# Second layer of a two-MLP kernel: 34 sets by seven block products instead of 17, one written order per kind of set, its weights decoded earlier

## The chip, the cores and the metric

The kernel runs on one core of a Trainium2 chip. The time is the device time of one execution in microseconds (us). The kernel before took 1127.06 us in the median of three runs (1126.33 to 1127.07). The engines are named as in the profile: PE (TensorE), PEld (its weight loads), DVE (VectorE), ACT (ScalarE), POOL (GpSimd) and SP (the engine whose queue starts most DMAs).

## What is computed

```python
def reference(**kw):
    X = np.fft.rfft(x, axis=1)                       # x: 2 x 3008 x 256
    x = np.fft.irfft(X * (filt_r + 1j * filt_i)[None], n=3008, axis=1)
    x = x.reshape(6016, 256)
    gate = 1.0 / (1.0 + np.exp(-(x @ moe_w_gate)))   # 256 -> 1536
    x = (gate * (x @ moe_w_val)) @ moe_w_out         # 1536 -> 256
    h = x @ moe2_w_in                                # 256 -> 2048
    return (h / (1.0 + np.exp(-1.702 * h))) @ moe2_w_out   # 2048 -> 256
```

A spectral filter comes first, then a gated layer (the first layer), then a layer with a sigmoid-GELU (the second layer). The weights arrive as float64 and are decoded on the chip.

## The kernel before

Precision: every fp32 operand is split into a high part (an fp32r copy, made by ACT) and a low part (the rest, made by a subtraction on POOL or DVE). `mm3` (lines 127 to 130) multiplies two split operands with three matmuls: high by high, high by low, low by high. A "product" below means these three matmuls, on a 128x128 block of weights and up to 512 columns of tokens.

Second layer: the 6016 tokens are twelve column tiles, ten of 512 and two of 448 columns (`tiles2`), taken as six pairs (p = 0 to 5). The 2048 hidden features are eight double blocks of 256 (fp = 0 to 7). A set is one pair p with one double block fp, so there are 48 sets. Into the hidden features each set goes by seven products instead of eight, P0 to P6 in the order P0, P4, P5, P1, P6, P2, P3 (`prod` in the loop, from line 1990 on): a Strassen-Winograd scheme, whose sums of weights and of tokens are made ahead. They lie in PSUM banks x (products 0, 5, 6, 3), y (4, 2) and z (1). ACT copies out c1 (from x) and c5 (from y). DVE then makes y = x + c5 (line 2011, here called Ay), z = z + c1 (line 2013, Az) and w = x + c5 (line 2025, Aw), and x is complete after P3. The GELU of z, w, y and x follows on ACT, once rounded (the high part) and once in full, and then the low part.

Out of the hidden features a set goes in one of two ways. A regular set (R) uses eight products (`Block.back`). A set by seven (S, class `Seven`, line 1817 on) uses seven, m1 to m7, with more sums: T1 = y - z, T3 = w - y, T2 = w - T1, T4 = x - T2, each split again into high and low. Of the seven, m3, m2 and m4 add into the accumulators. The products m1, m6, m7 and m5 go one after the other into one more bank, the chain, and after each DVE adds the chain into a sum in SBUF (k1 to k4, lines 1884 and 1886). At the end of a pair the sums are folded into the accumulators (`fold`, line 1919). `SETS7` names the sets by seven: fp 0, 2, 4, 6 in pairs 2 to 4, fp 4 and 6 in pair 1, fp 0, 2, 4 in pair 5, none in pair 0, which makes 17. Each is followed by an R set. The products of a set's second half are spread over the next set's first half.

Other work in this layer ("side steps") is taken from a list at places of the loop (`spend`, `rate`): the token forms of the next pair (four subtractions on DVE, seven high parts on ACT, seven low parts on DVE), the sums of output weights for the S sets (`out_sums`), and in pair 0 what is left of the decoding of the weights. The engines run their instructions in the order in which the program issues them; PE, DVE, ACT and POOL each go by this written order.

First layer: pairs p = 2 to 5 are run as twelve sets each by seven products in and eight out (line 1560 on). Decoding of the second layer's weights (`decode_chores`, 13 jobs here) begins in pair 4 and goes on into the second layer's pair 0.

Of the kernel before, what the change touches and what calls it, by code (L numbers as in the profile page):

```python
# [17 lines left out]
P = 128  # L18
# [71 lines left out]
def kernel(  # L90
# [29 lines left out]
    ascr = dram.tile([2, P, P], F32, name="ascr")  # L120

# [91 lines left out]
    def decode_chores(j, st, place):  # L213
# [4 lines left out]
        def start():  # L218
            t["raw"], _, _, own = raws.pop(0)
            slots.append(own)  # L220
            t["lw"], t["hw"] = t["raw"][:, :, 0], t["raw"][:, :, 1]
            ex = st.tile([P, 512], U32, tag="ex", name="ex")
            nc.vector.tensor_single_scalar(ex, t["hw"], 0x7FF00000, op=ALU.bitwise_and)
            t["c"] = st.tile([P, 512], I32, tag="c", name="c")
            nc.scalar.activation(out=t["c"], in_=ex, func=AF.Relu, bias=ebias, scale=8.0)
            t["m"] = st.tile([P, 512], U32, tag="m", name="m")
            nc.vector.tensor_scalar(t["m"], t["hw"], 0xFFFFF, 0x100000, op0=ALU.bitwise_and, op1=ALU.bitwise_or)
# [14 lines left out]
        def value():  # L242
            nc.vector.scalar_tensor_tensor(
                out=t["f"], in0=t["f"], scalar=2.0**-20, in1=t["c"].bitcast(F32), op0=ALU.mult, op1=ALU.mult
            )
            nc.scalar.activation(out=hi, in_=t["f"], func=AF.Copy)
# [34 lines left out]

        low.apart = end.apart = True
        return [start, mant, sign, value] + ([low] if j % 2 else [lambda: sums(0), low, lambda: sums(1), end])
# [899 lines left out]
    OUT = {(1, 0): 4, (1, 1): 6, (1, 2): 0, (1, 7): 2}  # L1183
# [290 lines left out]
    def forms_chores(dst, n, raws, spread, ahead, eng4=nc.vector):  # L1474
        def make():
            fs = Forms(dst, n, raws, spread, [st.tile([P, 512], F32, tag=k, name="xs") for k in ("ex", "c", "m")])
            cell.append(fs)
            one, two, three, four = fs.sums(eng4)
            if len(ahead) == 7:
                ks = (0, 1, 4, 5, 2, 6, 3)  # L1480
                steps = [one, two, three, four, lambda: fs.hi(0)]
                for k, nxt in zip(ks, ks[1:]):
                    steps += [lambda k=nxt: fs.hi(k), lambda k=k: fs.lo(k)]
                return steps + [lambda: fs.lo(3)]
# [33 lines left out]
    def l1_back(t, f, c, gp):  # L1518
# [3 lines left out]
        def run():  # L1522
            mm3(acc, [w[:, f, c * P:(c + 1) * P] for w in wo], [g[:, :n] for g in gp], f == 0, f == FC1 - 1)
            if f == FC1 - 1:
# [3 lines left out]
                evac(o[:, c, :n], acc, c)  # L1528
# [14 lines left out]
    def next_decode(j):  # L1543
        return decode_chores(j, st, lambda: [w[:, j % NWL] for w in wl] + [sp])

    def spend(q, n):
        for k in range(n):
            if not q and bulk and not hold_back:
                q.extend(next_decode(bulk.pop(0)))
            elif not q and out_jobs:  # L1550
                q.extend(out_sums(out_jobs.pop(0)))
# [8 lines left out]
    for p in range(FIRST, nt // 2):  # L1560
        n = tiles[2 * p][3]
        rhs = [[h[:, :n] for h in d] for d in sets[p]]
        for f in range(FC1):
# [32 lines left out]
            rate = (1, 0, 2) if first_set else RATE[p] if p == FIRST or f > 2 else (0, 2, 1) if f else (0, 0, 1)  # L1596
# [94 lines left out]
    frees = list(gring)  # L1691

    spares = []

    def gtake():
        return frees.pop(0)

    def give(slot, p):
        if p and slot is gring[0]:
            assert not spares  # L1700
            spares.extend(work.tile([P, 512], F32, tag=f"g{i}", name="spare", bufs=4) for i in range(2))
        else:
            frees.append(slot)

# [7 lines left out]
    class Block:  # L1712
        def __init__(self, i, j, p, fp, bank):
            self.i, self.j, self.t, self.fp, self.bank = i, j, 2 * p + j, fp, bank
            self.n = tiles2[self.t]
            self.own = p == 0 and i == 0 and (fp > 0 or j == 0)
            self.sg = None

        def take(self):
            self.slot = gtake()  # L1720
            self.gp = [x[:, :self.n] for x in self.slot]

        def hold(self):
            self.sg = work.tile([P, 512], F32, tag="sg", name="sg")[:, :self.n]
            return self.sg

        def act(self):
            self.take()
            if self.own:
                self.sg = self.bank  # L1730
            elif self.sg is None:
                self.hold()
            nc.scalar.activation(out=self.gp[0], in_=self.bank, func=AF.Gelu_apprx_sigmoid)  # L1733
            nc.scalar.activation(out=self.sg, in_=self.bank, func=AF.Gelu_apprx_sigmoid)  # L1734

        def full(self):
            nc.scalar.activation(out=self.bank, in_=self.bank, func=AF.Gelu_apprx_sigmoid)  # L1737
            self.sg = self.bank

        def high(self):  # L1740
            self.take()
            nc.scalar.activation(out=self.gp[0], in_=self.sg, func=AF.Copy)

        def low(self, eng=None):
            eng = eng or (nc.vector if self.own else nc.gpsimd)
            eng.tensor_sub(self.gp[1], self.sg, self.gp[0].bitcast(F32))  # L1746

        def back(self, c):
            t, n, f = self.t, self.n, 2 * self.fp + self.i
            end = self.fp == FC2 // 2 - 1 and self.i != self.j  # L1750
            acc = accs[self.j][c][:, :n]
            mm3(acc, wp(f, c), self.gp, opens(t, c), end, skip_group_check=True)
            if c:
                give(self.slot, now[0])
            if end:
                if c == 0:
                    outs[t, 2] = new_raw()
                o = outs[t, 2][:, c, :n]
                if c == 1 and t == nt - 2:
                    h = n // 2  # L1760
                    nc.scalar.copy(o[:, :h], acc[:, :h])
                    nc.scalar.dma_start(out=out[c * P:(c + 1) * P, pos2[t]:pos2[t] + h], in_=o[:, :h])
                    nc.vector.tensor_copy(o[:, h:], acc[:, h:])
                    nc.sync.dma_start(out=out[c * P:(c + 1) * P, pos2[t] + h:pos2[t] + n], in_=o[:, h:])
                    return
                evac(o, acc, c)
                (nc.scalar if t == nt - 1 and c == 0 else nc.sync).dma_start(
                    out=out[c * P:(c + 1) * P, pos2[t]:pos2[t] + n], in_=o
                )

    sout = [
        [wo[i][:, FC1 - 1, :P] for i in range(2)],
        [wo[i][:, FC1 - 1, P:] for i in range(2)],
        [sx0[i][:, 5, :] for i in range(2)],
    ]

    def load_sout(fp, *ks):
        q = SEVEN.index(fp)
        for k in ks:
            for i in range(2):  # L1780
                nc.sync.dma_start(out=sout[k][i].bitcast(F32), in_=oscr[q, i, :, k * P:(k + 1) * P])

    def out_sums(fp):
        w = slot(2 * fp + 1)
        q = SEVEN.index(fp)
        one, two = ("ex", "c") if q % 2 == 0 else ("c", "ex")
# [21 lines left out]
        def low():  # L1808
            if fp not in SETS7[nt // 2 - 1]:
                for i in range(2):  # L1810
                    nc.sync.dma_start(out=ascr[i], in_=w[i][:, P:2 * P].bitcast(F32))
            lo = st.tile([P, 512], F32R, tag=one, name="wlo")
            nc.vector.tensor_sub(lo, t["r"].rearrange("p k m -> p (k m)"), t["hi"].bitcast(F32))
            for i, x in enumerate((t["hi"], lo)):
                nc.sync.dma_start(out=oscr[q, i], in_=x[:, P:].bitcast(F32))
                nc.sync.dma_start(out=w[i][:, P:2 * P].bitcast(F32), in_=x[:, :P].bitcast(F32))

        steps = [lambda fn=fn: fn() for fn in (whole, sums, more, high, low)]
        for step in steps:
# [283 lines left out]
```

## Time and profile of the kernel before

| what | value |
|---|---|
| median of three runs | 1127.06 us |
| profiled execution | 1128.34 us, of which the span from the first to the last instruction is 1126.5 us |
| PE busy | 1117.2 us, 99% of the span, 5021 matmuls |
| DVE, ACT, POOL busy | 835.4, 672.8, 442.3 us |
| granted TensorE clock | 0.999 of full speed over the whole span |
| second layer on PE | from 644.5 to about 1122.5 us |

Matmuls overlap: a matmul of 512 columns is shown as 0.39 us long, but in a dense stretch the next one starts 0.227 us after it. DVE and ACT instructions overlap in the same way by about 0.1 us. So the time that PE loses is read from the distances between starts of matmuls, not from the busy share.

### The profile page before, as it was taken

Reading aid. Unit: us, or ns where it says so; the run is one execution under the profiler, and the core shown is the slowest. Engines: PE = TensorE matmul, PEld = TensorE weight load, DVE = VectorE, ACT = ScalarE, POOL = GpSimd, SP = SyncE. Lnnn points to the kernel's source line nnn. Section 1 sums busy time; section 2 is a strip of 40 time slices with the busy share of each in tenths; the row PEclk is TensorE's granted clock in tenths of the full one; section 3 lists DMA queues with packets and bytes.
Section 4 is the critical chain, followed back from the end, with each engine's and each line's share of the span. In section 5 each row is a group of like instructions: output and inputs, shape, how many; then the busy total and the mean of one; then the engine's idle time right before and its main releaser. Section 6 shows DMA issues by size and latency. Waiting matters only on the chain.

```text
span 1126.5 us, 15228 instructions
## 1 busy us (share of the span) xinstructions
PE 1117.2 (99%) x5021; PEld 895.8 (80%) x5021; DVE 835.4 (74%) x1395; ACT 672.8 (60%) x1276; POOL 442.3 (39%) x368
## 2 busy tenths in 40 slices
PE   9999999999999999999999999999999999999998
PEld 4378887767888888888888878888788888888897
DVE  6989997777688755787788789657876676776653
ACT  4555555554455544655565576667676666676664
POOL 3810003654333211211211132256566665666564
PEclk9999999999999999999999999999999999999999
DMA  8755238794300210026057251031030120210200
GB/s 208 202 183 182 94 113 220 184 194 85 94 1 1 70 41 1 19 108 126 1 184 246 85 183 39 1 117 47 15 116 20 43 75 15 85 29 20 66 15 33
DMA packets 101582, 100.29 MB, mean 89 GB/s; under 512 B 41024, under 2 KB 73536, under 8 KB 101504
## 3 DMA queue, kind: packets, MB, share of 16 engines
q1 hardware_dynamic: 99536, 96.42, 30.2%
q10 hardware_dynamic: 1968, 2.91, 0.8%
q8 instruction: 39, 0.64, 0.2%
q14 instruction: 39, 0.32, 0.1%
HBM read 62.34 MB, written 32.51 MB: 84 GB/s over the span
## 4 chain that ended last, share of the span: by engine, by line
PE 90%; DVE 2%; DMA 1%; ACT 1%; SPq 1%; POOL 1%; issue 1%; ACTq 0%; DVEq 0%; POOLq 0%
PE ps L128 30%; PE ps L130 29%; PE ps L129 29%; PE ps L328 2%; DMA fi<-in_fd_dram 0%; SPq L377 0%; DMA yraw<-tt 0%; DMA x<-in_xd_dram 0%; POOL g L1746 0%; DMA f<-fi 0%; DVE z L504 0%; ACT sg L1734 0%; DVE yp L1136 0%; SPq L363 0%; ACT ps L1737 0%
## 5 line engine op out<-in xcount | busy, mean ns | idle before, releaser
L1746 POOL TENSOR_TENSOR g<-sg,g 128x512 fp32r<-128x512 f32 (+1 forms) x82 | 113.2, 1382 | 141.9 <-ACT sg L1734 109.7
L125 POOL TENSOR_TENSOR g<-sg,g 128x512 fp32r<-128x512 f32 (+1 forms) x47 | 59.5, 1267 | 257.2 <-ACT g L124 257.2
L128 PE MATMUL ps<-yp,wg 128*128 128x512 f32 (+2 forms) x382 | 149.8, 393 | 0.0
L130 PE MATMUL ps<-yp,wg 128*128 128x512 f32 (+2 forms) x382 | 147.8, 387 | 0.0
L129 PE MATMUL ps<-yp,wg 128*128 128x512 f32 (+2 forms) x382 | 147.7, 387 | 0.0
L129 PE MATMUL ps<-g,wo 128*128 128x512 f32 (+1 forms) x305 | 117.4, 386 | 0.0
L128 PE MATMUL ps<-g,wo 128*128 128x512 f32 (+1 forms) x305 | 117.4, 386 | 0.0
L130 PE MATMUL ps<-g,wo 128*128 128x512 f32 (+1 forms) x305 | 117.3, 386 | 0.0
L1746 POOL TENSOR_TENSOR wo<-sg,wo 128x512 fp32r<-128x512 f32 (+1 forms) x65 | 89.1, 1371 | 64.6 <-ACT sg L1734 56.3
L128 PEld LDWEIGHTS ps<-yp,wg 128*128 128x128 f32 x382 | 71.7, 188 | 26.1 <-issue 13.0
L130 PEld LDWEIGHTS ps<-yp,wg 128*128 128x128 f32 x382 | 71.7, 188 | 14.3
L129 PEld LDWEIGHTS ps<-yp,wg 128*128 128x128 f32 x382 | 71.7, 188 | 13.1 <-issue 0.2
L1733 ACT ACTIVATE g<-ps 128x512 fp32r<-128x512 f32 (+1 forms) x73 | 43.1, 591 | 61.1 <-DVE ps L2013 58.0
L1637 ACT ACTIVATE sg<-ps 128x480 f32<-128x480 f32 (+1 forms) x48 | 28.1, 586 | 71.0 <-DVE ps L1635 71.0
L1671 DVE TENSOR_TENSOR g<-ps,g 128x480 fp32r<-128x480 f32 (+1 forms) x48 | 32.4, 675 | 48.8 <-ACT g L1668 48.6
L128 PEld LDWEIGHTS ps<-g,wo 128*128 128x128 f32 x305 | 57.2, 188 | 11.6 <-issue 0.8
L130 PEld LDWEIGHTS ps<-g,wo 128*128 128x128 f32 x305 | 57.2, 188 | 11.1
L129 PEld LDWEIGHTS ps<-g,wo 128*128 128x128 f32 x305 | 57.2, 188 | 10.9
L1734 ACT ACTIVATE sg<-ps 128x512 f32<-128x512 f32 (+1 forms) x103 | 60.5, 587 | 0.2 <-POOL g L1746 0.2
L2011 DVE TENSOR_TENSOR ps<-ps,tabs 128x512 f32<-128x512 f32 (+1 forms) x48 | 32.9, 685 | 37.0 <-PE ps L130 36.7
L128 PE MATMUL ps<-yp,sx 128*128 128x512 f32 (+2 forms) x129 | 50.2, 389 | 0.1
L1656 ACT ACTIVATE sg<-ps 128x480 f32<-128x480 f32 (+1 forms) x48 | 28.1, 586 | 37.2 <-PE ps L130 37.0
(372 smaller groups left out, 3144.3 us busy)
## 6 DMA issues: line engine op xcount, KB each, us to landing
yscr<-tt SPq DMA_DIRECT2D x56, 128.0 KB, 2.2
raw<-in_w_out_dram SPq DMA_DIRECT2D x14, 512.0 KB, 4.0
yraw<-xscr SPq DMA_DIRECT2D x14, 512.0 KB, 5.2
x<-in_xd_dram SPq DMA_DIRECT2D x32, 192.0 KB, 3.8
wscr<-wl SPq DMA_DIRECT2D x24, 256.0 KB, 2.0
wg<-wscr SPq DMA_DIRECT2D x24, 256.0 KB, 2.9
out_dram<-yraw SPq DMA_DIRECT2D x20, 256.0 KB, 2.1
f<-in_fd_dram SPq DMA_DIRECT2D x23, 192.0 KB, 4.3
```

The source lines that it names most:

```text
L125: lo_eng.tensor_sub(dst_lo, src, dst_hi.bitcast(F32))
L128: nc.tensor.matmul(out=o, lhsT=w[0], rhs=x[0], start=first, stop=False, **kw)
L129: nc.tensor.matmul(out=o, lhsT=w[0], rhs=x[1], start=False, stop=False, **kw)
L130: nc.tensor.matmul(out=o, lhsT=w[1], rhs=x[0], start=False, stop=last, **kw)
L328: nc.tensor.matmul(out=o[c], lhsT=w[64 * r:64 * r + n], rhs=x(r, k), start=True, stop=True, tile_position=(64 * r, 64 * k),)
L1637: nc.scalar.activation(out=sgz, in_=z, func=AF.Sigmoid)
L1656: nc.scalar.activation(out=sgy, in_=y, func=AF.Sigmoid)
L1671: nc.vector.tensor_sub(g0[1], x, g0[0].bitcast(F32))
L1733: nc.scalar.activation(out=self.gp[0], in_=self.bank, func=AF.Gelu_apprx_sigmoid)
L1734: nc.scalar.activation(out=self.sg, in_=self.bank, func=AF.Gelu_apprx_sigmoid)
L1746: eng.tensor_sub(self.gp[1], self.sg, self.gp[0].bitcast(F32))
L2011: nc.vector.tensor_add(y, x, s5[:, :n])
```

## The change

1. `SETS7` becomes fp 0 to 5 in pair 1 and fp 0 to 6 in pairs 2 to 5: 34 sets, most of them one behind the other. The block sums of output weights are made for seven double blocks (`OUT`: six in pair 0, the seventh in pair 1), and there is a second buffer for those that an S set loads (`souts`).
2. The loop of the second layer is rewritten. Each set is a table of single steps (`Set.ops`), and five written lines (`LINES`) give the order in which steps of the set before (with a "-"), of the current set, of the pair's end and side steps (aD, aA, aQ: the next one for DVE, ACT, POOL) are issued. The key is the kinds of the two sets: SS is an S set after an S set. One line covers one "frame": what is issued between one set's start and the next's. In names like `zhi`, `zf`, `zlo`: high part, full value, low part; `xf-` is that of the set before.
3. The low parts of the token forms move from DVE to POOL (`lo_eng`, aQ). At the end of a pair, POOL adds two pairs of sums (V, W), and DVE adds accumulator and sum into the output tile (e11 to e22).
4. The second layer's weights are decoded from pair 3 of the first layer on (its fourth), not pair 4; one job of thirteen is left for the second layer. ACT's table for GELU is called for ahead of the second layer.

The core of the diff:

```diff
-    SEVEN = (0, 2, 4, 6)
-    SETS7 = {1: (4, 6), 2: SEVEN, 3: SEVEN, 4: SEVEN, 5: (0, 2, 4)}
+    SEVEN = tuple(range(FC2 // 2 - 1))
+    SETS7 = {0: (), 1: (0, 1, 2, 3, 4, 5), 2: SEVEN, 3: SEVEN, 4: SEVEN, 5: SEVEN}
-    OUT = {(1, 0): 4, (1, 1): 6, (1, 2): 0, (1, 7): 2}
+    OUT = {(0, 2): 0, (0, 3): 1, (0, 4): 2, (0, 5): 3, (0, 6): 4, (0, 7): 5, (1, 7): 6}
...
-            if p == 3 and f == 10:
+            if p == 3 and f == 0:
                 raw_job(EARLY)
-            if p == 4 and f == 0:
                 raw_job(EARLY + 1)
+            if p == 3 and f == 1:
                 bulk += range(EARLY, NJ)
-            hold_back = p == 4 and f > 7 or p == 5 and f > 6
+            hold_back = p in (3, 4) and f > 7 or p == 5 and f > 7
...
+    gelu(warm, ebias)
+    LINES = {
...
+        "RS": (
+            "P0 bz0- bz1- c1 P4 xf- P5 c5 xlo- aQ P1 Ay bw1- ylo- aQ V W Az P6 zf P2 Aw bw0- yf bx1- T1 whi aA aA "
+            "bx0- wf e21 zhi P3 e11 by0- T2 xhi by1- T3 aD e22 e12"
+        ),
+        "SS": (
+            "zlo- xf- wlo- P0 T1hi- P4 T2hi- c1 m1- T2lo- T4- c5 xlo- m3- T3hi- aA k1- aD P5 T4hi- T3lo- aQ P1 Ay "
+            "m6- T1lo- Az P6 k2- zhi P2 zf Aw m7- T4lo- yf m2- whi k3- wf P3 T1 m5- T3 xhi T2 m4- k4-"
+        ),
...
+            ops["Ay"], ops["Az"], ops["Aw"] = add(y, x, c5), add(z, z, c1), add(f["w"], x, c5)
+            gelu_of("z", "z", z, f["z"], pool)
+            gelu_of("w", "w", f["w"], f["w"], pool)
+            if self.seven:
+                so = souts[nseven % 2]
+                nseven += 1
+                for k in (2, 0, 1):
+                    for i in range(2):
+                        nc.sync.dma_start(out=so[k][i].bitcast(F32), in_=oscr[fp, i, :, k * P:(k + 1) * P])
+                gelu_of("x", "x", x, x, vec)
+                ops["yf"] = lambda: gelu(y, y)
+                ops["T1"], ops["T3"] = sub(vec, f["t1"], y, f["z"]), sub(vec, f["e0"], f["w"], y)
+                ops["T2"], ops["T4"] = sub(vec, f["t2"], f["w"], f["t1"]), sub(vec, f["e1"], x, f["t2"])
+                for k, name, src, eng in (
+                    ("t1", "T1", "t1", pool), ("t2", "T2", "t2", pool), ("t3", "T3", "e0", pool), ("t4", "T4", "e1", vec)
+                ):
+                    split_of(k, name, f[src], eng)
...
+    def forms_side(sets, n, raws):
+        fs = Forms(sets, n, raws, False, temps)
+        one, two, three, four = fs.sums()
+        steps = [("D", one, None), ("D", two, one), ("D", three, one), ("D", four, two)]
+        need = {0: None, 4: one, 5: two, 1: None, 6: three, 2: None, 3: four}
+        for k, fn in need.items():
+            hi = lambda k=k: fs.hi(k)
+            steps += [("A", hi, fn), ("Q", lambda k=k: fs.lo(k, nc.gpsimd), hi)]
         return steps
...
+            if fp == 2 and p + 1 < nt // 2:
+                todo += forms_side(setB if p % 2 else setA, tiles2[2 * p + 2], raw2)
+            frame(LINES[prev.kind + cur.kind], cur, prev, ends if fp == 0 else None)
```

## Rows read from the trace of the kernel before

**Rows 1.** The page, its first part: busy time of each engine.
```profile
PE 1117.2 (99%) x5021; PEld 895.8 (80%) x5021; DVE 835.4 (74%) x1395; ACT 672.8 (60%) x1276; POOL 442.3 (39%) x368
```
**Rows 2.** Stretches: length, busy us (instructions) by engine, clock, DMA share, GB/s.
```profile
469.00:559.00 90.00, 89.96 (x397) 74.06 (x396) 69.89 (x120) 52.80 (x93) 17.95 (x14) 1.00 0.32 79
644.50:727.00 82.50, 82.33 (x361) 67.04 (x361) 65.99 (x100) 57.30 (x108) 23.57 (x17) 1.00 0.23 76
727.00:808.00 81.00, 79.76 (x348) 64.58 (x347) 55.56 (x80) 50.61 (x94) 42.59 (x33) 1.00 0.20 62
```
**Rows 3.** Timeline of PE: start, length, engine, line, operation, tiles.
```profile
1017.98 0.39 PE L128 MATMUL ps<-sx,wg 128*128 128x512 f32 x1
...
1028.86 0.39 PE L128 MATMUL ps<-sx 128*128 128x512 f32 x1
...
1085.44 0.36 PE L128 MATMUL ps<-wo,wg 128*128 128x448 f32 x1
...
1086.05 0.36 PE L128 MATMUL ps<-wo,wg 128*128 128x448 f32 x1
...
1122.32 0.37 PE L130 MATMUL ps<-wo,wl 128*128 128x448 f32 x1
```
**Rows 4.** Timeline of all engines around a stop of PE in pair 1.
```profile
792.45 1.29 POOL L1746 TENSOR_TENSOR g<-sg,g 128x512 fp32r<-128x512 f32 x1 [2.95 <-PE ps L130]
...
792.92 1.37 DVE L1136 TENSOR_TENSOR sx<-xs,sx 128x512 fp32r<-128x512 f32 x1 [1.08 <-ACT sx L1131]
...
794.02 0.39 PE L130 MATMUL ps<-wo,wg 128*128 128x512 f32 x1
794.21 0.68 DVE L2025 TENSOR_TENSOR sg<-ps,tabs 128x512 f32<-128x512 f32 x1
...
794.94 0.50 PE L128 MATMUL ps<-xk,wl 128*128 128x512 f32 x1 [0.54 <-DVE sg L2025]
795.28 0.39 PE L129 MATMUL ps<-xk,wl 128*128 128x512 f32 x1
```
**Rows 5.** Timeline of POOL and DVE at two near-simultaneous starts.
```profile
695.70 1.29 POOL L1746 TENSOR_TENSOR g<-sg,g 128x512 fp32r<-128x512 f32 x1 [1.76 <-ACT sg L1734]
...
695.73 1.54 DVE L227 TENSOR_SCALAR m<-raw 128x512 uint32<-128x512 uint32 x1
...
818.47 0.69 DVE L1843 TENSOR_TENSOR sg<-sg 128x512 f32<-128x512 f32 x1
818.51 1.80 POOL L1746 TENSOR_TENSOR wo<-sg,wo 128x512 fp32r<-128x512 f32 x1 [0.65 <-ACT wo L1742]
```
**Rows 6.** Timeline from Az to POOL's low part of z, with Aw.
```profile
832.98 0.68 DVE L2013 TENSOR_TENSOR ps<-ps,s 128x512 f32<-128x512 f32 x1
...
833.58 0.68 DVE L1154 TENSOR_TENSOR xs<-yraw,xs 128x512 f32<-128x512 f32 x1
833.69 0.39 PE L130 MATMUL ps<-sx,wo 128*128 128x512 f32 x1
833.70 0.60 ACT L1733 ACTIVATE g<-ps 128x512 fp32r<-128x512 f32 x1 [3.13 <-DVE ps L2013]
...
834.19 0.69 DVE L2025 TENSOR_TENSOR sg<-ps,tabs 128x512 f32<-128x512 f32 x1
834.19 0.59 ACT L1734 ACTIVATE sg<-ps 128x512 f32<-128x512 f32 x1
...
834.86 1.30 POOL L1746 TENSOR_TENSOR g<-sg,g 128x512 fp32r<-128x512 f32 x1 [3.56 <-ACT sg L1734]
```
**Rows 7.** Timeline: c5 and the high part after it; a chain product and its sum.
```profile
821.34 0.60 ACT L2003 COPY tabs<-ps 128x512 f32<-128x512 f32 x1
...
821.81 0.67 ACT L1742 ACTIVATE g<-spare 128x512 fp32r<-128x512 f32 x1
...
825.47 0.39 PE L130 MATMUL ps<-g,wo 128*128 128x512 f32 x1
...
825.90 0.69 DVE L1884 COPY sums<-ps 128x512 f32<-128x512 f32 x1 [0.24 <-PE ps L130]
```

More of the change, by code (lines that the diff above doesn't have):

```diff
@@ L1689 @@
     gn[0] = 0
[L1691 to L1703, printed above, removed]
     opened = set()
@@ L1710, in opens @@
         return new
[L1712 to L1781, printed above, removed]
+    def gelu(o, x):
+        nc.scalar.activation(out=o, in_=x, func=AF.Gelu_apprx_sigmoid)
+    LAST = FC2 // 2 - 1
@@ new lines, in out_sums @@
+        return [("D", whole), ("D", sums), ("D", more), ("A", high), ("D", low)]
+    late = ctx.enter_context(tc.tile_pool(name="late", bufs=1))
+    temps = [late.tile([P, 512], F32, name=f"temp{k}") for k in range(3)]
+    seen = {}
+    while chores:
+        chore(chores)
+    assert len(bulk) == 1 and len(queue) == 1
+    gelu(warm, ebias)
+    LINES = {
+        "BR": (
+            "P0 q0- c1 L0- P4 h0- c5 h1- L1- P5 Ay P1 Az zhi h2- zf P6 zlo Aw h3- P2 yhi whi yf wf P3 wlo xhi"
+        ),
[6 more added lines that the diff above has]
+            "m6- T1lo- Az P6 k2- zhi P2 zf Aw m7- T4lo- yf m2- whi k3- wf P3 T1 m5- T3 xhi T2 m4- k4-"
+        ),
+        "SR": (
+            "wlo- xf- zlo- P0 xlo- aD P4 c1 T4- aD aD m3- T2hi- c5 aA P5 T2lo- m1- T3hi- aA Ay aD P1 T3lo- k1- "
+            "T1hi- P6 Az m6- T1lo- Aw zhi P2 T4hi- k2- zf P3 T4lo- whi zlo m7- wf m2- k3- wlo aQ m4- xhi m5- yf "
+            "yhi k4-"
+        ),
+        "RR": (
+            "aA aD aQ P0 bz1- bz0- c1 ylo- P4 xf- P5 c5 xlo- bw0- Ay aD bw1- P1 P6 Az aD by0- Aw aD aD aD zhi P2 "
+            "zf bx0- zlo aQ yf aA bx1- whi wf aA P3 wlo by1- yhi xhi"
+        ),
+    }
@@ new lines, in job_side, with frame @@
+    def job_side(steps):
+        before, last_job[:] = last_job[0], [steps[-1][1]]
+        return [(e, fn, steps[i - 1][1] if i else before) for i, (e, fn) in enumerate(steps)]
+    def frame(line, cur, prev, ends):
+        for tok in line.split():
+            if tok in ("aD", "aA", "aQ"):
+                side(tok[1])
+            elif tok.endswith("-"):
+                prev.ops.pop(tok[:-1], lambda: None)()
+            elif cur and tok in cur.ops:
+                cur.ops.pop(tok)()
+            elif ends:
+                ends.ops.pop(tok, lambda: None)()
@@ L2025 @@
-            nc.vector.tensor_add(bw.bank, x, s5[:, :n])
-            if bz.own:
-                bz.low()
-            bw.act()
-            bw.low()
-            if fold:
-                fold(3)
-            prod(y, 2, False)
-            if seven:
-                by.full()
-            back()
-            back()
-            if seven:
-                seven.after_y()
-            else:
-                by.act()
-                if was and was.last:
-                    was.fold(0)
-                    folds = was.fold
-                spend(chores, rate[2])
-                by.low()
@@ L2046 @@
-            prod(x, 3, False)
-            if seven:
-                seven.after_x()
-            else:
-                bx.act()
-                bx.low()
-            back()
-            back()
-            if seven:
-                held = seven.backs()
-            else:
-                blocks = (bz, bw, by, bx) if fp or p == 0 else (bw, bz, by, bx)
-                held = [lambda o=o, c=c: o.back(c) for o in blocks for c in range(2)]
-    queue += held
-    while queue:
-        back()
+                assert 2 * fp in done and {2 * fp, 2 * fp + 1} <= placed and fp in summed
@@ L2064 @@
+            assert fp or p < 3 or len(todo) < 2
+            frame(LINES[prev.kind + cur.kind], cur, prev, ends if fp == 0 else None)
+            prev = cur
+        ends = Ends(p)
+    assert not todo
+    frame("xf- ylo- xlo- V W bz0- bz1- bw0- bw1- fold by0- e12 by1- e22 bx0- e11 bx1- last", None, prev, ends)
 def kernel(**inputs):
```

357 lines of the change are left out of this document (164 added, 193 removed).

## The prediction

> **What bounds the kernel now.** I read three views in this order. The first part of the page: PE is busy 99% of the span, DVE 74%, ACT 60%, POOL 39% [rows 1], so only fewer matmuls, or fewer stops of PE, shorten the kernel. Then the table of stretches: the clock is at its upper level (1.00) in each stretch shown, and in pair 0 (644.5 to 727) and pair 1 (727 to 808) of the second layer PE is busy nearly throughout [rows 2]. The clock I leave as it is: no stop below is longer than 0.7 us. Last the timeline, because the busy share hides short stops: matmuls of 512 columns start 0.2267 us apart when dense (48 of them between the two rows, 10.88 us), those of 448 columns 0.2033 us apart (three in 0.61) [rows 3]. A product of three matmuls is 0.68 us, or 0.61.
>
> How much PE loses in the second layer: 48 sets of 45 matmuls less 17 x 3 are 2109. Pairs 0 to 4 have 1758 of them, 398.5 us; pair 5 has 351, 71.4 us; some 15 left over from the first layer add about 3.3. Dense, that is 473.2 us. The layer runs from 644.5 [rows 2] to 1122.32 + 0.20 [rows 3], 478.0 us. So 4.8 us are lost.
>
> One such loss shows what the change can meet. At 792.45 POOL begins a subtraction of 1.29 us. At 792.92 DVE begins one whose two inputs are both in SBUF. It takes 1.37 instead of about 0.69 us and ends at 794.29, 0.55 us after POOL's end (793.74). The next DVE instruction, Aw, begins only at 794.21, and PE, whose next matmul was due at 794.25, begins at 794.94; its first step is 0.34 instead of 0.227 long [rows 4]. So a stop costs its length plus 0.11 us, here 0.80 in all. Who starts first wins: with a lead of 0.03 us POOL held DVE up (1.54 us); with a lead of 0.04 us DVE passed in 0.69 and POOL took 1.80 [rows 5]. So the two share something that one of them holds at a time; I call it the port. DVE subtractions with one input in PSUM (Ay, Az, Aw, T1, T3, T4, xlo) keep 0.68 to 0.70 us, as Aw does at 834.19 [rows 6]. In the changed order, those with both inputs in SBUF are T2, T4lo and the four token sums (aD).
>
> **The saving.** 17 more sets by seven take away one product each. Pair 1 gains 4, pairs 2 to 4 three each, pair 5 four: 13 x 3 x 0.2267 = 8.8 us and 4 x 3 x 0.2033 = 2.4 us, together 11.3 us, all on PE's path. The old stops go with the old order. I count 3.8 of the 4.8 us as gone and leave 1.0 for the transitions between kinds; the bounds are 0 and 4.8. Saving: 15.1 us.
>
> **What the new order costs: the SS frame.** There are 29 frames of an S set after an S set (fp 1 to 5 in pair 1, fp 1 to 6 in pairs 2 to 5). Dense, a frame is 14 products, 9.52 us, against 10.2 for a regular one. DVE has 13 steps in it, one per 0.60 us (832.98 to 833.58 [rows 6]): 7.8 us, which fits. POOL has five of 1.3 us and ACT 13 of about 0.5. So no engine is full by its sum; what counts is when the steps meet. I place them by the written order, t = 0 at P0. A product ends at its place times 0.68. DVE starts 0.43 us after the last matmul's start (825.47 to 825.90 [rows 7]), or 0.50 for a step that also has to wait for another engine (Aw, 833.69 to 834.19 [rows 6]).
>
> Frames with token sums (16: fp 2 to 5 in pairs 1 to 4, one aD, aA and aQ in each). k1 follows m1 (its last matmul starts at 1.81): 2.24. aD is the next DVE step: 2.84. On ACT c5 starts at 1.55, T3hi 0.47 later and takes 0.67 [rows 7], so POOL's T3lo starts 0.08 after its end (834.19 + 0.59 to 834.86 [rows 6]), at 2.77. POOL leads by 0.07, so aD waits until 4.06 and ends at 4.61. Ay, due at 3.67, is done at 5.22; P6, due at 4.76, writes the bank that Ay reads and starts at 5.27. That is a stop of 0.51 + 0.11 = 0.62 us. Worked on into the next frame, POOL is late with wlo, T2 waits for it, k1 slips, and the stop is 0.73. If DVE leads instead, T3lo, the aQ and T1lo each shift back, T4lo waits for T1lo until 7.3, k3 ends at 8.45, and m5 (due at 8.16), which overwrites the bank that k3 reads, stops by 0.24 + 0.11 = 0.35. The port's own sum says the same: six POOL steps of 1.26 and three DVE steps of 0.6 are 9.4 of 9.52 us. So the bounds are 0.35 and 0.73 and I take the middle, 0.54: 16 x 0.54 = 8.6 us.
>
> Frames without side steps (10: fp 1 in pairs 1 to 4, fp 1 to 6 in pair 5). Az starts at 4.28 and POOL's zlo 1.88 later (832.98 to 834.86 [rows 6]): 6.16. Aw starts at 5.71, T4lo is next: 6.31. POOL leads by 0.15. T4lo then waits until 7.45, ends at 8.00, k3 ends at 8.61, and m5 starts at 8.66 instead of 8.16: 0.50 + 0.11 = 0.61 us. At 448 columns the same steps, shrunk by 448/512, give a lead near 0.1 us and about the same stop. Two more waits in front of zhi than before (its old slot is still read by m1 and by POOL) could each take back about 0.07 us of the lead, as the two latencies above differ by 0.07. The bounds are 0 and 10 x 0.61 = 6.1; I take half, 3.0 us. The three frames with only an aQ (fp 6, pairs 2 to 4) have T1lo ahead of T4lo, which waits 0.35 us and makes k3 no later than m5 allows: nothing.
>
> **Costed at nothing.** Decoding from pair 3 on: pair 4 ran the same rates with decoding under it at 89.96 of 90 us PE busy [rows 2]; if that cover fails at pair ends, 1 us. The loads of the 17 further sets (six blocks each on SP's queue, behind the output stores) are issued a frame ahead into a second buffer; if one is late, m3, m6 or m7 waits, as no trace shows here. The low parts of the forms on POOL (aQ) are counted above. V, W and e11 to e22 replace the folds under 15 products of the RS frame; if T2 there waits for zlo, P4 of the next frame stops by 0.33 us in five pairs: 0 to 1.7. The end (last product, two half copies, store) stays.
>
> **The sum.** 15.1 - 8.6 - 3.0 = 3.5 us less. The profiled execution took 1128.34 us (span 1126.5 and 1.8 around it), 1.28 above the median; the difference is the same for both, so 1124.8 for such an execution and 1127.06 - 3.5 = 1123.5 for the median. A measurement of this kernel can tell about 0.2%, 2.3 us, from no change.
>
> **The rivals.**
> 1. No meeting costs anything: DVE leads everywhere and the slack of the chain takes the rest. 1127.06 - 15.1 = 1112 us. For it: before, in the 17 S sets, T2 (line 1843) led POOL by 0.04 us [rows 5] as in the one shown. Against it: port time of 9.4 in 9.52 us. The Trainium skill, Advanced Engine Details and Errata, section VectorE Performance Modes, names only two-port instructions of VectorE as those that block GpSimd and are blocked; by that alone a two-input fp32 subtraction would pass and this time would hold. The trace disagrees (1.37 instead of 0.69 us [rows 4]), as does SBUF — State Buffer, section Who interferes with whom, which counts two SBUF inputs too.
> 2. Every meeting costs its full price: 16 x 0.73 + 6.1 + 1.3 for RS frames = 19.1 us, 1127.06 - 15.1 + 19.1 = 1131 us; with one of the groups milder, 1127 to 1131. For it: in both groups POOL leads by more than the 0.03 us that sufficed [rows 5].
> 3. DVE falls behind through the sums: T2 waits for wlo to beyond 0.66 us into the next frame; k4 comes after it, and m1 (due at 1.36), which overwrites the chain, stops as well by about 0.22 + 0.11 = 0.33 us in each frame with token sums. 16 x 1.06 + 6.1 + 1.3 = 24.4 us, 1136 us, slower. For it: wlo starts near 9 in such frames and T2 at 9.4 to 9.6. Against it: T2 ended at 0.37, 0.63 and 0.55 in the frames I placed with POOL leading.
> 4. The sets by seven are there, but a load or a weight sum comes late and PE waits for it in some sets: 1120 to 1130.
>
> **How the numbers follow.** Forecast (1119 to 1126): 0.45, of which 0.36 is faster by over 0.2% and 0.09 within. Rival 1 (1111 to 1118): 0.16, faster. Rival 2 (1127 to 1131): 0.20, of which 0.14 within and 0.06 slower. Rival 3 (1131 to 1139): 0.15, slower. Rival 4: 0.04, a quarter each way and half within. Faster 0.53, same 0.25, slower 0.22. The range from 1112 to 1132 leaves out the lower part of rival 1 (0.06) and most of rival 3 (0.13). The forecast alone spans 1119 to 1126.
>
> **What would show it.** 4970 matmuls instead of 5021. In pairs 1 to 4, fp 2 to 5: a line-1142 type subtraction of over 1 us under a POOL step, then a distance of about 0.8 us between two matmuls ahead of P6; frames of about 10.1 us. In pair 5 the same ahead of m5, behind a long T4lo. If the SS frames are 9.5 us long, rival 1 holds; if PE also stops ahead of m1, rival 3. A stop at first-layer pair ends or on a DMA would make the part costed at nothing wrong.

## The result and the profile after

The changed kernel took 1141.63 us (median of four runs, 1140.19 to 1143.77), the kernel before 1127.07 in the runs beside it: a ratio of 1.0132, interval [1.0114, 1.0149]. So it is 14.6 us slower, where 3.5 us faster was forecast, and it lies beyond every rival and outside the range (1112 to 1132). The profiled execution took 1143.77 us, its span is 1142.0.

First part of the page, as [rows 1]: busy us, share of the span, instructions.
```profile
PE 1117.4 (98%) x4970; PEld 886.2 (78%) x4970; DVE 922.6 (81%) x1519; ACT 702.6 (62%) x1317; POOL 545.9 (48%) x444
```
The 51 matmuls are gone (5021 to 4970), and yet the span has grown. The table of stretches, as [rows 2]:
```profile
469.00:559.00 90.00, 89.96 (x397) 74.04 (x396) 69.82 (x120) 52.66 (x93) 17.93 (x15) 1.00 0.32 80
644.50:727.00 82.50, 81.09 (x356) 65.97 (x355) 47.63 (x73) 52.32 (x97) 50.07 (x36) 1.00 0.23 76
727.00:808.00 81.00, 74.21 (x311) 58.55 (x310) 71.98 (x97) 54.33 (x100) 57.42 (x41) 0.98 0.22 69
965.00:1044.00 79.00, 77.25 (x333) 61.85 (x332) 70.67 (x101) 58.63 (x108) 63.35 (x48) 1.00 0.20 60
```
Pair 1 is where PE loses most (79.76 to 74.21 us busy in 81), and of these stretches it alone has a granted clock below 1.00. The first layer is as before (89.96 of 90); under the earlier decoding the lag behind the kernel before grows only from 0.90 us (at 332 us, the same matmul by number) to 0.95 (at 645). Who ends PE's waits, in us, times, longest; the lines 1831, 1878 and 1828 are DVE's additions, first copies of the chain into a sum, and subtractions of the new `Set`:
```profile
PE ps L126 <- DVE ps L1831: 9.5, 18, 2.1
PE ps L126 <- DVE sums L1878: 1.6, 4, 0.4
PE ps L126 <- DVE sums L1831: 1.6, 4, 0.4
PE ps L126 <- DVE fulle L1828: 1.3, 4, 0.4
```
Read from the distances of matmuls, as in the prediction (what lies beyond the dense distance, the slow first step with it), PE loses 28.1 us in the second layer, against 4.3 before. That is +23.8, and the products save 11.3: 12.5 of the 15.5 us that the span grew. Of the rest, 0.95 us is a later first layer, of which 0.91 stands already at 227 us, ahead of the first load for the earlier decoding (304 us); 0.7 is a longer end (4.9 instead of 4.2 us from the last matmul's start), and about 1.2 is dense distances that are a little longer in the mean (0.2275 against 0.2271 us with 512 columns, 0.2041 against 0.2027 with 448), whose cause is open.

Five readings show where the stops come from. A meeting is a step of DVE and one of POOL that want the port at the same time; a stop is what PE loses. The idle time in brackets counts from the end of the last record; at 512 columns PE's loss by distances is 0.27 us more (0.16 because a record is longer than the dense distance, 0.11 for the slow first step).

The stop ahead of P6 in a frame with token sums, around 852 us; all engines: start, length, engine, line, operation, tiles.
```profile
850.76 1.30 POOL L1828 TENSOR_TENSOR g<-fulle,g 128x512 fp32r<-128x512 f32 x1 [0.22 <-ACT g L1834]
850.85 1.75 DVE L1156 TENSOR_TENSOR temp<-yraw,temp 128x512 f32<-128x512 f32 x1
...
852.53 0.68 DVE L1831 TENSOR_TENSOR ps<-ps,tabs 128x512 f32<-128x512 f32 x1
852.54 0.39 PE L128 MATMUL ps<-wo,wo 128*128 128x512 f32 x1
...
853.27 0.50 PE L126 MATMUL ps<-sx,wo 128*128 128x512 f32 x1 [0.34 <-DVE ps L1831]
853.61 0.39 PE L127 MATMUL ps<-sx,wo 128*128 128x512 f32 x1
```
This is the forecast's picture: POOL's T3lo leads by 0.09 us (0.07 worked out), aD ends 0.54 us after POOL, Ay is late, and P6 loses 0.62 us (853.27 - 852.54, and 0.34 to the next, less 2 x 0.227).

The stop ahead of m5 in a frame without side steps:
```profile
833.83 1.30 POOL L1828 TENSOR_TENSOR g<-sg,g 128x512 fp32r<-128x512 f32 x1 [1.87 <-ACT sg L1711]
833.91 1.76 DVE L1828 TENSOR_TENSOR ks<-fulle,ks 128x512 fp32r<-128x512 f32 x1
...
835.59 0.68 DVE L1878 COPY sums<-ps 128x512 f32<-128x512 f32 x1
...
836.33 0.50 PE L126 MATMUL ps<-g,wg 128*128 128x512 f32 x1 [0.42 <-DVE sums L1878]
```
zlo leads T4lo by 0.08 us; k3 is late, and m5 loses 0.69.

Weight sums in pair 1. `OUT` starts six jobs in pair 0, but the aD places there are too few, and the rest runs in pair 1's frames ahead of the token sums:
```profile
763.52 1.30 POOL L1828 TENSOR_TENSOR g<-fulle,g 128x512 fp32r<-128x512 f32 x1 [0.21 <-ACT g L1834]
...
763.64 1.34 DVE L1740 TENSOR_TENSOR wr<-wv 128x128 f32<-128x128 f32 x1
...
764.78 1.33 POOL L1146 TENSOR_TENSOR sx<-yraw,sx 128x512 fp32r<-128x512 f32 x1
...
764.90 1.37 DVE L1741 TENSOR_TENSOR wr<-wv,wr 128x128 f32<-128x128 f32 x1
...
766.19 0.68 DVE L1831 TENSOR_TENSOR ps<-ps,tabs 128x512 f32<-128x512 f32 x1
...
766.93 0.50 PE L126 MATMUL ps<-yp,wo 128*128 128x512 f32 x1 [1.19 <-DVE ps L1831]
```
These two subtractions have a quarter of the columns (0.28 us undisturbed, median of seven), but one aD issues both, and each meets a POOL step and takes 1.34 and 1.37. The price of a meeting is what is left of POOL's step, not the size of DVE's. P6 loses 1.46 us.

The end of pair 1. The token sums, pushed back by the weight sums, end in the frame of fp 6, the SR line:
```profile
794.26 1.37 POOL L1828 TENSOR_TENSOR wo<-fullt,wo 128x512 fp32r<-128x512 f32 x1 [0.43 <-ACT wo L1834]
...
794.39 0.68 DVE L1828 TENSOR_TENSOR fulle<-ps,fullt 128x512 f32<-128x512 f32 x1
...
794.99 1.19 DVE L1160 TENSOR_TENSOR yraw<-yraw 128x512 f32<-128x512 f32 x1
...
795.78 1.52 POOL L1828 TENSOR_TENSOR g<-fulle,g 128x512 fp32r<-128x512 f32 x1 [0.16 <-PE ps L128]
...
796.10 1.76 DVE L1164 TENSOR_TENSOR temp<-yraw,temp 128x512 f32<-128x512 f32 x1
...
797.78 0.69 DVE L1831 TENSOR_TENSOR ps<-ps,tabs 128x512 f32<-128x512 f32 x1
```
PE around it, and the stretch after it:
```profile
796.04 0.39 PE L128 MATMUL ps<-yp,wl 128*128 128x512 f32 x1
798.52 0.50 PE L126 MATMUL ps<-yp,sx 128*128 128x512 f32 x1 [2.09 <-DVE ps L1831]
...
799.53 0.63 PE L126 MATMUL ps<-wo,sout 128*128 128x512 f32 x1
799.96 0.63 PE L127 MATMUL ps<-wo,sout 128*128 128x512 f32 x1
```
```profile
799.30:802.00 2.70, 2.70 (x8) 2.11 (x7) 2.00 (x4) 2.21 (x5) 0.57 (x1) 0.50 0.00 0
```
The step at 794.39 has one input in PSUM and keeps 0.68 us under POOL's step; the two aD behind it, with both inputs in SBUF, are held. Two held aD in a row make a wait of 2.09 us, and shortly after it the granted clock is 0.50, the lower level, 1.2 GHz: matmuls start 0.43 us apart until about 802.5. The whole costs 3.97 us, 2.36 the wait with its slow first step and 1.6 the clock.

The RS line, behind a regular set:
```profile
736.36 1.29 POOL L1828 TENSOR_TENSOR g<-sg,g 128x512 fp32r<-128x512 f32 x1 [3.98 <-PE ps L128]
736.41 1.79 DVE L1828 TENSOR_TENSOR fullt<-sg,fullt 128x512 f32<-128x512 f32 x1
...
738.12 0.68 DVE L1828 TENSOR_TENSOR fulle<-sg,ps 128x512 f32<-128x512 f32 x1
738.72 1.18 DVE L1749 TENSOR_TENSOR wlo<-wr,wh 128x512 fp32r<-128x512 f32 x1
738.85 0.50 PE L126 MATMUL ps<-yp,wg 128*128 128x512 f32 x1 [0.36 <-DVE fulle L1828]
...
739.82 1.28 DVE L1909 COPY yraw<-ps 128x512 f32<-128x512 f32 x2
...
741.15 0.51 PE L126 MATMUL ps<-wo,sx 128*128 128x512 f32 x1 [0.64 <-DVE yraw L1909]
```
T2 loses its start by 0.05 us and holds up T3, for which P4 waits; then a step of the weight sums is held up as well, e22 and e12 come late, and m3 waits for the accumulator.

### The profile page after: what moved, and what is told of

Same layout as the page of the kernel before. It is cut to its first block, busy times and chain, and to the rows that moved or that the text cites. A ratio compares the mean times of both kernels' runs of the same rounds, so it can differ in the third digit from the quotient of the medians.

```text
span 1142.0 us, 15709 instructions
## 1 busy us (share of the span) xinstructions
PE 1117.4 (98%) x4970; PEld 886.2 (78%) x4970; DVE 922.6 (81%) x1519; ACT 702.6 (62%) x1317; POOL 545.9 (48%) x444
## 4 chain that ended last, share of the span: by engine, by line
PE 80%; DVE 11%; issue 3%; ACT 1%; DMA 1%; POOL 0%; SPq 0%; POOLq 0%; DVEq 0%; ACTq 0%
PE ps L126 27%; PE ps L128 26%; PE ps L127 26%; PE ps L338 2%; DVE fullt L1828 2%; DVE ps L1831 2%; DVE fulle L1828 1%; DVE sums L1831 1%; DVE sg L1831 1%; DVE ks L1828 1%; DVE sums L1878 1%; DMA yraw<-tt 0%; DVE g L1828 0%; DVE yraw L1907 0%; DVE wlo L1749 0%
## 5 line engine op out<-in xcount | busy, mean ns | idle before, releaser
L123 POOL TENSOR_TENSOR g<-sg,g 128x512 fp32r<-128x512 f32 (+1 forms) x47 | 59.5, 1267 | 257.3 <-ACT g L122 257.3
L1711 ACT ACTIVATE g<-ps 128x512 fp32r<-128x512 f32 (+1 forms) x110 | 63.9, 588 | 107.8 <-DVE ps L1831 91.2
L1828 POOL TENSOR_TENSOR g<-sg,g 128x512 fp32r<-128x512 f32 (+1 forms) x48 | 70.7, 1474 | 58.2 <-ACT sg L1711 29.3
L1831 DVE TENSOR_TENSOR sums<-sums,ps 128x512 f32<-128x512 f32 (+1 forms) x116 | 77.5, 668 | 12.8 <-PE ps L128 12.4
L1828 POOL TENSOR_TENSOR g<-fulle,g 128x512 fp32r<-128x512 f32 (+1 forms) x61 | 79.5, 1309 | 15.4 <-ACT g L1834 7.5
L1828 POOL TENSOR_TENSOR wo<-sg,wo 128x512 fp32r<-128x512 f32 (+1 forms) x48 | 64.2, 1337 | 23.0 <-ACT sg L1711 15.9
L1649 ACT ACTIVATE sg<-ps 128x480 f32<-128x480 f32 (+1 forms) x48 | 28.1, 586 | 68.5 <-DVE ps L1647 68.5
L127 PEld LDWEIGHTS ps<-g,wo 128*128 128x128 f32 x305 | 57.2, 188 | 11.3 <-DVE g L1683 0.4
L1828 POOL TENSOR_TENSOR wo<-fullt,wo 128x512 fp32r<-128x512 f32 (+1 forms) x34 | 44.2, 1300 | 36.2 <-ACT wo L1834 36.2
```

What stands on the lines that cost most here:

```text
L123: lo_eng.tensor_sub(dst_lo, src, dst_hi.bitcast(F32))
L127: nc.tensor.matmul(out=o, lhsT=w[0], rhs=x[1], start=False, stop=False, **kw)
L1649: nc.scalar.activation(out=sgz, in_=z, func=AF.Sigmoid)
L1711: nc.scalar.activation(out=o, in_=x, func=AF.Gelu_apprx_sigmoid)
L1828: return lambda: eng.tensor_sub(o, a, b)
L1831: return lambda: vec.tensor_add(o, a, b)
```

## The experiments

Theory A is the port of the prediction: VectorE's steps with two inputs in SBUF and POOL's steps hold each other up, and what PE loses follows from where the written line puts them. The rivals stand in each expectation. Ratios are to the kernel before, run beside each; the changed kernel's is 1.0132.

**POOL only writes.** Each subtraction of POOL in the second layer, and V and W, become a write of zeros, so the low parts and those pair sums are left out.
```diff
-                return lambda: eng.tensor_sub(o, a, b)
+                if eng is nc.gpsimd:
+                    return lambda: eng.memset(o.bitcast(F32), 0.0)
...
```


> The changed kernel, in which POOL writes zeros in the second layer where it subtracts or adds (the low parts, the pair's sums): left out are those low parts and sums. A write of a constant reads nothing in SBUF. Theory A (DVE steps with both inputs in SBUF wait for the port that a POOL subtraction holds, and PE then waits for DVE): the stops of PE ahead of P6, m5, P4 and m3 in pairs 1 to 5 vanish, the second layer is dense but for under 3 us, 1114 to 1119 us. Theory B (the written order is too tight by itself: 13 or 14 DVE steps in a frame of 9.5 us, taken strictly in order): at least half of the stops stay, above 1128 us.

1112.04 us, ratio 0.9865 [0.9851, 0.9880], a little below what A said (1114 to 1119); PE's stops in the second layer sum to 0.98 us. The loads, the weight sums, ACT's order and the decoding are all there still, so none of them costs PE anything as long as POOL holds nothing up. But a write takes 0.53 us instead of 1.3, so POOL is also faster. Two runs part these causes.

**Three writes for one.** The same with three writes for each subtraction.


> As the run in which GpSimd only wrote zeros (1112.0), but with three such writes for each subtraction, so that GpSimd is busy at least as long per step as in the changed kernel (3 x 0.53 = 1.6 us less what they overlap, against 1.3); low parts and the two pair sums are left out as there. Theory A (a lock that both hold only while they read SBUF by two ports): 1111 to 1115, VectorE's long subtractions stay at 0.68 to 0.70. Rival (in the first run it was GpSimd's speed that helped: its low parts simply came earlier): the stops come back at least in part, over 1122.

1112.18 us, 0.9871 [0.9855, 0.9887]. POOL is now at least as long at its steps as in the changed kernel (1.69 us for three), and DVE runs under it undisturbed: after 727 us no DVE step takes over 0.9 us. Below, six writes in a row. Timeline of POOL and DVE:
```profile
844.93 3.34 POOL L1829 MEMSET wo<- 128x512 f32 x6
...
845.50 0.68 DVE L1830 TENSOR_TENSOR ks<-fulle,ks 128x512 fp32r<-128x512 f32 x1
```
So it is not how long POOL works. One reserve stays: the writes don't wait for GELU's outputs and so begin earlier.

**POOL copies.** The full value is copied where the high part was subtracted from it, and V and W become copies, so the low parts and those pair sums are left out; but a copy of a GELU output waits for it as the subtraction did.
```diff
+                if eng is nc.gpsimd:
+                    return lambda: eng.tensor_copy(o, a)
...
```


> GpSimd copies the full value (one input from SBUF, one output) where it subtracted the high part from it; the low parts are therefore the full values, and the result is not that of the reference. It waits for the same GELU outputs. Theory A in its narrow form (only two-input steps take the lock): 1111 to 1116 if the copy is no longer than the subtraction, VectorE's long subtractions at 0.7. In its wide form (any GpSimd step that reads SBUF takes it): 1125 or more, with VectorE steps of over 1 us left. The rival (GpSimd's speed) gives 1135 or more if a copy takes 1.3 us.

1112.54 us, 0.9868 [0.9854, 0.9883]. By the time this is the narrow form, by the trace the wide one:
```profile
847.33 0.62 POOL L1829 CAST g<-sg 128x512 fp32r<-128x512 f32 x1 [3.56 <-ACT sg L1711]
847.49 1.00 DVE L1830 TENSOR_TENSOR ks<-fulle,ks 128x512 fp32r<-128x512 f32 x1
```
A copy with one input holds DVE up too: DVE's step ends again 0.54 us after POOL's, but the copy takes 0.62 us, so the step loses 0.32 us instead of 1.08, and the order's slack takes that. My expectation had put 1.3 us for the copy, which was a guess. So in these runs it is POOL's reading of SBUF that holds DVE up, and the length of the hold sets the price. The Trainium skill, SBUF — State Buffer, section Who interferes with whom, says the same: two SBUF inputs on VectorE contend with a GpSimd instruction that reads SBUF, not with one that only writes it. The traces agree (0.68 us under writes, 1.00 under a copy, 1.76 under a subtraction in the changed kernel).

**No token sums.** The four aD subtractions of each pair are left out; the steps that split the sums take other tokens in their place.
```diff
-        one, two, three, four = fs.sums()
+        one, two, three, four = (lambda k=k: None for k in range(4))
+        fs.src.update({4: fs.b12, 5: fs.b22, 6: fs.b12, 3: fs.b21})
```


> The changed kernel without the four DVE subtractions that make the token sums of the next pair (left out; the splits read the raw tokens instead). Theory A: the stops ahead of P6 in frames fp 2 to 5 of pairs 2 to 4 (12 of 0.5 to 0.6 us) vanish, and those of pair 1 that come from these steps, the last of 4.0 us above all; those ahead of m5, P4 and m3 stay: 11 to 12 us less than the changed kernel, 1129 to 1132 us. Theory B: 20 of some 600 DVE steps are gone, at most 0.6 us of DVE time each and not in the frames of pair 5, where PE stops as well: under 5 us less, above 1136 us.

1127.49 us, 1.0009 [1.0000, 1.0018], lower than A said (1129 to 1132). Gone are all stops ahead of P6 in pairs 2 to 4, the 3.97 us at the end of pair 1 with the lower clock (1.00 there), and one of 1.96 us in pair 0 that I had not ascribed to them; the sum is 14.6 us. Pair 1 keeps 0.92, 1.47, 1.50 and 0.60: these belong to the weight sums. The stops ahead of m5 and in the RS line stay.

**wlo first.** In the SS line zlo- and wlo- change places, so that POOL's zlo doesn't stand in front of T4lo.
```diff
-            "zlo- xf- wlo- P0 T1hi- ...
+            "wlo- xf- zlo- P0 T1hi- ...
```


> The changed kernel with two POOL steps exchanged in the SS line: wlo before zlo. Theory A: POOL is idle when T4lo starts, so the eight stops ahead of m5 (0.67 us each, 5.4 us) vanish; zlo now ends about 1.1 to 1.6 us into the next frame, and m1, due at 1.36, stops by up to 0.4 us in some frames: 2 to 5 us less than the changed kernel, 1137 to 1140 us. Theory B: PE gets neither low part too late today, so exchanging them changes nothing or costs: 1141 us or more, and the stops ahead of m5 stay.

1138.99 us, 1.0097 [1.0080, 1.0114]. All stops ahead of m5 go, those ahead of P6 shrink to 0.38 to 0.50 us in pairs 2 to 4, and one of about 0.3 us in m1, which waits for zlo, appears in 24 of the 29 SS frames; the end of pair 1 stays as it was, with the lower clock. That is 26.3 us in sum. The meeting was the cause of the m5 stops; moving the step moves the loss.

**Pair 1 with five sets by seven.** The sixth weight sum moves to pair 1's end.
```diff
-    SETS7 = {0: (), 1: (0, 1, 2, 3, 4, 5), 2: SEVEN, ...
+    SETS7 = {0: (), 1: (0, 1, 2, 3, 4), 2: SEVEN, ...
-    OUT = {... (0, 6): 4, (0, 7): 5, (1, 7): 6}
+    OUT = {... (0, 6): 4, (1, 6): 5, (1, 7): 6}
```


> The changed kernel with five sets by seven in pair 1, not six (33 in all); the sums of output weights for the sixth double block are made in pair 1, after its S sets, not at the end of pair 0. One product more: 0.68 us. Theory A with its consequence (the left-over steps of the sixth weight sum run among pair 1's S sets, where each two-input step meets a POOL step, and they push the token sums to the pair's end): the stops of 1.5 us ahead of P6 in pair 1 fall to 0.6 and the one of 4.0 us at its end to under 1: 4 to 6 us less than the changed kernel, 1136 to 1138 us. Rival: pair 1 is slow because it has no sums yet to fold and starts its S sets from POOL's backlog: its stops stay, 1142 us.

1134.82 us, 1.0069 [1.0054, 1.0084]: one set fewer by seven, and 6.8 us faster, a little more than the 4 to 6 expected. Pair 1's stops ahead of P6 are about 0.6 us each, and its end has neither the wait nor the lower clock; 21.7 us of stops are left. In these lines the thirty-fourth set saves 0.68 us of products and costs 6.8 in the balance.

**T3 ahead of T2 in the RS line.**
```diff
-            "bx0- wf e21 zhi P3 e11 by0- T2 xhi by1- T3 aD e22 e12"
+            "bx0- wf e21 zhi P3 e11 by0- T3 xhi by1- T2 aD e12 e22"
```


> The changed kernel with one line altered: in the line between a set by eight and a set by seven, T3 is written ahead of T2, and e12 ahead of e22. T3 reads one operand from PSUM, T2 two from SBUF, so T2 alone can meet GpSimd's lock. Theory A: the stop of about 0.6 us ahead of P4 behind T3 at the start of the pairs 1 to 4 (738.10, 826.52, 908.22, 989.05 in the changed kernel) goes, and the stop of 0.9 us ahead of m3 behind e12 shrinks or stays where e12 still comes after a T2 that waits; together 1 to 3 us, 1138.5 to 1140.5. Theory B (the RS frame is short of VectorE time whatever its order): the stops stay in sum within 0.5 us, 1141 to 1142.

1139.48 us, 1.0104 [1.0090, 1.0118]; its interval overlaps the changed kernel's, so the trace decides. The stops behind T3 are gone in all pairs, m3 still waits for e12 (0.99 and 0.94 us), and a new one of 0.42 follows it twice: 26.7 us in sum, 1.4 less.

**Another order.** Four of the five lines (RS, SS, SR, RR) are written anew, with the same operations, sets and buffers: the aim is that no two-input step of DVE behind which PE waits comes just after the start of a POOL step; token and weight sums are spread over more frames. The SS line:
```diff
-            "zlo- xf- wlo- P0 T1hi- P4 T2hi- c1 m1- T2lo- T4- c5 xlo- m3- T3hi- aA k1- aD P5 T4hi- T3lo- aQ P1 Ay "
-            "m6- T1lo- Az P6 k2- zhi P2 zf Aw m7- T4lo- yf m2- whi k3- wf P3 T1 m5- T3 xhi T2 m4- k4-"
+            "zlo- aA wlo- xf- P0 m1- T4- xlo- aQ m3- c1 P4 T2hi- P5 T3hi- k1- c5 P1 T2lo- m6- aD Ay T1hi- Az P6 "
+            "T3lo- P2 T1lo- T4hi- k2- zf yf zhi m7- Aw T4lo- m2- whi P3 wf k3- xhi T1 m5- T3 k4- m4- T2"
```


> The changed kernel with another order in four of its five written lines (the same operations, 34 sets by seven, the same tensors and buffers): the lines were laid so that a two-input subtraction on VectorE or a split on GpSimd that will meet the other's lock has slack behind it, and the steps of token sums and weight sums are spread over more frames. Theory A (the locks cost time only where the written line puts a meeting ahead of something that TensorE needs at once): the 25 or so stops of 0.5 to 1.5 us go, as does the drop of the clock in pair 1, and the time falls by 22 to 27 us from 1141.6, to 1115 to 1120; VectorE's long subtractions stay as many as in the changed kernel, only nobody waits for them. Theory B (with 34 sets each frame has so many meetings that no line avoids them; a stop taken away at one place comes back at another): over 1127, with stops of TensorE of over 12 us in the second layer.

1115.93 us, ratio 0.9894 [0.9878, 0.9910]: faster than both kernels, 25.7 us below the changed one with the same 4970 matmuls and the same work. PE's stops sum to 1.9 us, and pair 1 is full:
```profile
727.00:808.00 81.00, 81.00 (x357) 66.29 (x356) 64.68 (x101) 57.87 (x107) 65.05 (x49) 1.00 0.21 66
```
The expectation that DVE's long steps stay as many was wrong. T2 by line, over its 34 executions (minimum, median, maximum in ns), first in the changed kernel, then in this one:
```profile
L1828 DVE TENSOR_TENSOR fullt<-sg,fullt x34: 610/1210/1786, 736.4 to 1123.0; 128x512 f32<-128x512 f32 x27, 128x448 f32<-128x448 f32 x7
```
```profile
L1828 DVE TENSOR_TENSOR fullt<-sg,fullt x34: 616/759/774, 734.9 to 1095.0; 128x512 f32<-128x512 f32 x27, 128x448 f32<-128x448 f32 x7
```
DVE instructions of over 1.0 us after 727 us fall from 60 to 14; POOL's of over 1.5 us go from 47 only to 43. So most meetings are now won by DVE, and what waits is POOL, for whose low parts PE doesn't stop. The new lines also move steps of PE and ACT; how much of the gain is won meetings and how much slack behind lost ones was not parted. An aD that still loses starts later under POOL's step and takes 1.06 instead of 1.75:
```profile
833.88 1.30 POOL L1828 TENSOR_TENSOR wo<-fullt,wo 128x512 fp32r<-128x512 f32 x1
...
834.66 1.06 DVE L1156 TENSOR_TENSOR temp<-yraw,temp 128x512 f32<-128x512 f32 x1
```

**A second order**, laid out independently from the same lines.


> A second, independent order of the same four lines, with the same sets and the same operations. Theory A as for the first: 1115 to 1121, because which line it is does not matter so long as no meeting stands ahead of an operand that is due. Theory B: over 1127, or far from the first one, which would say that the gain hangs on single chances of timing.

1116.44 us, 0.9909 [0.9896, 0.9922], with other meetings (26 DVE instructions of over 1.0 us) and 4.0 us of stops, half of it one stop behind a token sum that waits for its load until 901.43.

**33 sets and another order.**


> 33 sets by seven (five in pair 1, the sixth and seventh weight sums made in pair 1's last two frames) with an order found for these. One product of three matmuls more, 0.68 us. Theory A: within 1 us of the two with 34 sets, 1115 to 1121, since the thirty-fourth set brings 0.68 us only once its weight sums have room. Rival (the weight sums are what stands in the way, whatever the order): 4 us or more below the two with 34 sets, as was found between 34 and 33 sets in the written order of the change (1141.6 to 1134.8).

1116.05 us, 0.9903 [0.9887, 0.9918]: level with the two orders of 34 sets. With room in the lines the weight sums are no obstacle, and the 6.8 us between 34 and 33 sets in the change's own lines were the order's.

## Why the prediction was wrong

What it named is what happened; what it left at nothing decided. Stops in us:

| term of the sum (rounded) | forecast | measured |
|---|---|---|
| products removed | -11.3 | -11.3 (51 matmuls) |
| stops of before | 4.8, 1.0 to stay | 4.3; 0.4 stays at 650, the rest is in the rows below |
| frames with token sums, pairs 2 to 4 (12) | 6.5 | 7.0 (0.49 to 0.62 each) |
| stops ahead of P6 in pair 1 (5) | 2.2 (four) | 5.1 (0.59 to 1.49) |
| frames without side steps (10) | 3.0 | 5.4 (eight stops of 0.66 to 0.69) |
| RS frames | 0 (0 to 1.7) | 2.6 ahead of P4, 1.9 ahead of m3 |
| end of pair 1 | 0 | 4.0 |
| pair 0 | 0 | 2.0 |

- **The saving** held in its main term. Its second term (3.8 us for old stops) did not: the old stops went, but the places between kinds of sets got more in their stead.
- **Frames with token sums.** Right in pairs 2 to 4, in mechanism and size: 0.58 us on average against 0.54, within 0.35 to 0.73. The 0.54 itself was a middle between two cases, and only one came: POOL led in all twelve, by 0.09 to 0.12 us, for which 0.62 had been worked out (it came lower in pair 4, whose token sums have 448 columns). In pair 1 the step failed, because I counted one aD per frame as a token sum, and the prediction's list of steps with both inputs in SBUF (T2, T4lo, the token sums) left out those of the weight sums. The first places there go to weight sums left from pair 0, and one such aD issues two small two-input steps, both of which can meet. I had all I needed to see it: `OUT` starts six jobs in pair 0, and they are taken ahead of the token sums. The run without token sums and the run with five sets in pair 1 show it.
- **Frames without side steps.** The price was right (0.61 worked out, 0.66 to 0.69 found), the choice of half was not. The worked lead of 0.15 us came out as 0.08 (833.83 to 833.91), and 0.04 to 0.05 in pair 5, still more than the 0.03 of [rows 5], and eight of ten frames paid. The lead was the evidence; the half was only a hedge. One that paid nothing is pair 5's last, where the SR line begins with wlo-. The other is pair 1's first, whose stop came ahead of P6.
- **Costed at nothing.** This step failed most. The decoding cost nothing, as said. No wait for the new blocks of output weights shows. But V, W, e11 to e22 and T2 in the RS line were taken as 0, bounded at 1.7 us, and cost 4.5, since T2 itself meets zlo and e12 comes behind a blocked weight sum. Pair 0 cost 2.0: by the trace a blocked step of the weight sums (line 1741) delays ACT's copy of them, and ACT's GELU is queued behind it; as the stop is gone without the token sums too, it hangs on the order of both. And the end of pair 1 was not looked at.
- **"The clock I leave as it is: no stop below is longer than 0.7 us"** fell with that: a wait of 2.09 us was followed by the lower level, 1.6 us more.
- **The rivals.** No meeting costs anything, 1112, is what the kernel gives when POOL only writes (1112.04 and 1112.18) or holds for half as long (1112.54); as a price list it was exact. Full price, 1131, was the right mechanism, some 10 us short, for it had no terms for pair 0, the weight sums in pair 1, its end and e12. DVE falling behind through m1 is not what cost the time: no stop ahead of m1 is in the changed kernel; stops in m1 appear only when wlo goes first, and then for zlo. Late loads: none.
- **Two readings of rows.** The 1.54 us of [rows 5], from which the 0.03 us lead was taken, belong to a step with one input (`TENSOR_SCALAR`, line 227); the same step takes 0.42 us in 13 of its 16 executions. So steps with two inputs are not the only ones that POOL holds up; this kind lies in the decoding, and none runs after 727 us. And the row for Aw (834.19) has hardly any POOL step under it (0.02 us); that a step with one input in PSUM keeps 0.68 us is shown by the one at 794.39.
- **Forecast against result.** 28.1 us of stops against 12.6: 15.5 of the 18.1 us by which the median was missed. The rest lies in the first layer, the end and the mean dense distances, as above, and was not pursued.

## What to carry to other kernels

Where two engines share a port, the sum of busy times says little: with the same instructions, this kernel took 1141.6 or 1115.9 us by the order alone. List each step that can meet the other engine, side steps and leftovers of the stage before too; for each, who starts first, by how much, and who is waiting for what stands behind it. Give the lead or the slack to the step that the bounding engine waits for, and let the other lose.

## What the runs showed that was not expected

- A lead of 0.04 to 0.12 us decides the whole hold. A DVE step of 512 columns that lost ends some 0.55 us after POOL's end, whether POOL held for 0.62 us (a copy) or 1.30 (a subtraction); of 448 columns 0.48, of 128 columns 0.15.
- A DVE step of 128 columns, 0.28 us alone, took 1.34 under the same hold: it loses 1.06 us, a step of 512 columns 1.08.
- POOL instructions that only write hold no DVE step up, not even six in a row over 3.34 us.
- One wait of 2.09 us was followed by the clock at 0.50 for some 3 us, and so was the wait at the same place with wlo first (2.15) and with T3 ahead of T2 (2.11). A wait of 1.77 us in the second order was not (the first stretch below, from its trace), nor were two of 1.2 us in the changed kernel's pair 1 (one lies in the second stretch). Without the 2.09 us wait (no token sums, or five sets in pair 1) the clock stays at 1.00 there.
```profile
904.00:909.00 5.00, 4.96 (x22) 4.11 (x23) 4.41 (x7) 3.12 (x6) 3.79 (x3) 1.00 0.14 40
```
```profile
756.00:778.00 22.00, 20.47 (x88) 16.24 (x89) 21.65 (x31) 15.51 (x29) 15.82 (x12) 1.00 0.16 48
```
